# A retention-then-FFN kernel: one unit's transposes go from TensorE to the DMA queue, and loads, casts and a state sum change places

## The chip, the cores and the metric

The kernel runs on one core of a Trainium2 chip. The metric is the device time of one execution in microseconds. The kernel before was run three times: median 202.52 us, from 202.31 to 202.76. The profile shown comes from one further execution, which took 203.15 us; the span from its first to its last instruction is 201.4 us, so 1.75 us lie around the span.

A core has TensorE (matrix products, writes PSUM), VectorE (called DVE in the profile), ScalarE (ACT), GpSimd (POOL) and SyncE (SP, here used only to issue DMAs). POOL issues DMAs too: its queue is q0 in the profile, SP's is q1. The 16 DMA engines serve both. PSUM has 8 banks of 128 x 512 numbers in float32; the code writes each out by its number.

## The reference

A retention recurrence over 768 tokens, for 4 batches and 8 heads of size 64, and after it two matrix products with a PReLU between them, over all 4 x 768 = 3072 tokens:

```python
for t in range(S):
    state = gamma * state + einsum('bhd,bhe->bhde', k[:, :, t], v[:, :, t])
    y[:, :, t] = scale * einsum('bhd,bhde->bhe', q[:, :, t], state)
x = y.transpose(0, 2, 1, 3).reshape(3072, 512)
h = x @ w_in                                    # 512 x 2048
g = maximum(h, 0) + alpha * minimum(h, 0)
out = g @ w_out                                 # 2048 x 512
```

## The kernel before

**Units.** The recurrence is done in chunks. A unit is 256 tokens of one batch; there are 12, three to a batch, and two units make a block of 512 tokens for the FFN, so there are six blocks. A unit u goes through these steps, each a helper in the code:

- `load(u)` issues the DMAs of k, q and v on SP's queue into staging tiles `ks`, `qs`, `vs` (three buffers of each).
- `rescale(engine, u, t, h0, h1)` multiplies k (t=0) or q (t=1) of heads h0 to h1 by powers of the decay and writes `kdq` in float16. `cast_v` writes v in float16 as `vx`.
- `kdq` has tokens on the partitions; the scores need it turned. `turn_pe(u, hh, bank)` turns half of the heads with 8 TensorE transposes into a PSUM bank, and ACT copies the bank to `kq`. `turn_dma(u)` turns the whole `kdq` into `kq` with one transposing DMA on SP's queue. Units 0 to 3 use `turn_pe`, units 4 to 11 `turn_dma`.
- `score_mm(u, hh, banks)` makes the scores of half of the heads in two banks, `masks` (DVE) multiplies them by the causal mask into `m`, and thereby frees the banks.
- `sum_mm` makes the sums of k times v for each 128 tokens (tile `st`), `state_sum` (DVE, then POOL) adds one to the running state and applies the decay (tiles `ss`, `tf`), `state_copy` writes it in float16 as `tg` (ACT or POOL).
- `out_mm(u, banks)` makes the unit's output `y`: products of `tg` and `kq` (line 319) and of `m` and `vx` (line 339); `take_y` copies it to `xT`.

**FFN.** `ffn1(n, ...)` multiplies by w_in, turn after turn in the banks of its list, with ACT and DVE applying the PReLU (`hm`, then `gt`). For block 1 it is split: its first six turns need only unit 2 (the first 256 tokens), the later ones unit 3 too. Block 0 uses `ffn2`, which adds up w_out in four parts, one for each piece of w_out (`get_wo(0)` to `get_wo(3)`, cast on the way by DMAs that POOL issues). The later blocks use `ffn2_seven`, which makes the product from seven half-size ones (ox, oy, oz) and needs differences of w_out's quarters (`w_sums`, DVE) and of g's (`g_sums`, DVE).

**Order.** The schedule is manual: each engine runs its instructions in the order in which the code names them, and waits only for data or buffers. `ffn1` and `ffn2` are generators; `tick(gen, m)` issues the next m of their steps (matmuls, mostly), so the code weaves attention steps of the next units into the FFN. Dependencies beyond data are added by hand. `hold`, called by `load` for each whole DMA, makes the DMA wait for an instruction put on the list `held`. `behind` makes a POOL scaling wait for a named DVE instruction, the `gate`.

**Around the change** (lines 671 to 740, between the first FFN product of block 0 and the loop): POOL scales unit 2, then unit 2's scores, sums and masks are woven into `ffn2(0)`. Unit 3's load waits for the first mask of unit 2. The third piece of w_out is issued, and the load of unit 4 waits until it has landed. Unit 3 is scaled by DVE and POOL together, its v cast, and `turn_pe` for it stands inside the first half of `ffn1(1)`. The last w_out differences are the gate for the second scaling of unit 4; units 4 and 5 are then scaled and cast on POOL, and turned by DMA. In the loop, for u0 = 4, 6, ... the two units' sums and scores come first (lines 763 to 766), then the states and masks of u0 (767 to 772).

Of the kernel before, what the change touches and what calls it, by code (L numbers as in the profile page):

```python
# [21 lines left out]
def kernel(  # L22
# [106 lines left out]
    def load(u, parts="kqv"):  # L129
        b, c = divmod(u, UPB)  # L130
        t = staged.setdefault(u, {})
        for nm in parts:
            src = {"k": k, "q": q, "v": v}[nm[0]]
            if nm[0] not in t:
                t[nm[0]] = sbp.tile(
                    [128, H, 2 * D], FP, tag=f"{nm[0]}s", bufs=3, name=f"{nm[0]}s{u}"
                )
            h = slice(0, H) if len(nm) == 1 else slice(4 * int(nm[1]), 4 * int(nm[1]) + 4)
            if u >= SPLIT and nm != "q":
                for x in range(2):  # L140
                    for y in range(2):
                        at = U * c + 128 * x + 64 * y
                        nc.sync.dma_start(
                            out=t[nm][rows(x), :, D * y : D * y + D],
                            in_=src[b, :, at : at + 64, :].rearrange("h p d -> p h d"),
                        )
                continue
            hold(
                nc.sync.dma_start(  # L149
                    out=t[nm[0]][:, h, :],  # L150
                    in_=src[b, h, U * c : U * c + U, :].rearrange(
                        "h (p r) d -> p h (r d)", r=2
                    ),
                )
            )
# [10 lines left out]
    def rescale(eng, u, t, h0, h1):  # L166
        kdq = unit(u)[0]
        at = OQ if t else (O2 if u >= SPLIT else 0)
        return eng.tensor_tensor(  # L169
            out=kdq[:, t, :, h0:h1, :].rearrange("p r h d -> p h r d"),  # L170
            in0=staged[u]["kq"[t]][:, h0:h1, :].rearrange("p h (r d) -> p h r d", r=2),
            in1=tab[:, at + 2 * h0 : at + 2 * h1]
            .rearrange("p (h r) -> p h r", r=2)
            .unsqueeze(3)
            .to_broadcast([128, h1 - h0, 2, D]),
            op=MULT,
        )
# [115 lines left out]
    def masks(u, hh, parts=(0, 1)):  # L293
        for a in parts:
            m2 = sbp.tile([128, 512], F16, tag=f"m2{a}{hh}", bufs=2, name=f"m2{a}{hh}")
            if u >= SPLIT:
                i = nc.vector.tensor_tensor(
                    out=m2[:, 0:384], in0=live[u, hh][a][:, 0:384], in1=mj, op=MULT
                )
            else:  # L300
                i = nc.vector.tensor_tensor(  # L301
                    out=m2.rearrange("p (r a i) -> p r a i", r=2, a=2),
                    in0=live[u, hh][a].rearrange("p (r a i) -> p r a i", r=2, a=2),
                    in1=mask.unsqueeze(2).to_broadcast([128, 2, 2, 128]),
                    op=MULT,
                )
            live[u, hh][a] = m2
        return i
# [84 lines left out]
    def ffn1(n, banks, apart=0):  # L393


        gt = sbp.tile([128, NFT, TB], F16, tag="gt", bufs=2, name=f"gt{n}")
        gts[n] = gt
        turns = [(f, 2, ul, ul + 1) for ul in range(2) for f in range(0, apart, 2)]
        rest = range(apart, NFT)
        if apart == 0:  # L400
            rest = [f + x for f in range(HF) for x in (0, HF)]
        turns += [(f, 1, 0, 2) for f in rest]
        for i, (f0, nf, lo, hi) in enumerate(turns):
            hps = ps(banks[i % len(banks)], "hps").rearrange("p (f t) -> p f t", f=nf)
            for f in range(nf):
                for hp in range(4):
                    nc.tensor.matmul(  # L407
                        out=hps[:, f, :].rearrange("p (u t) -> p u t", t=U),
                        lhsT=w_in_all[:, hp, 128 * (f0 + f) : 128 * (f0 + f) + 128],
                        rhs=xT[n][:, lo:hi, hp, :],  # L410
                        start=(hp == 0),
                        stop=(hp == 3),
                    )
                    if f < nf - 1 or hp < 3:
                        yield
            hm = sbp.tile([128, TB], FP, tag="hm", bufs=3, name="hm")
            hm = hm.rearrange("p (f t) -> p f t", f=nf)
            nc.scalar.activation(out=hm, in_=hps, func=RELU, bias=0.0, scale=-1.0)  # L418
            for f in range(nf):
                nc.vector.scalar_tensor_tensor(  # L420
                    out=gt[:, f0 + f, U * lo : U * hi],
                    in0=hm[:, f, :],
                    scalar=oma_sb[:, f0 + f : f0 + f + 1],
                    in1=hps[:, f, :],
                    op0=MULT,
                    op1=ADD,
                )
            if n > 0 and f0 in ((HF + 3, NFT - 1) if apart == 0 else (NFT - 1,)):

                lo = 0 if apart or f0 < NFT - 1 else 4  # L430
                hi = HF if f0 == NFT - 1 else 4
                g_sums(n, 0, lo, hi)
                g_sums(n, 1, lo, hi)
            yield
# [146 lines left out]
    def get_wo(i):  # L581
        s = slice(4 * i, 4 * i + 4)
        return nc.gpsimd.dma_start(out=w_out_all[:, s, :], in_=wo[:, s, :])
# [88 lines left out]
    get_wo(1)  # L672
    rescale(G, 2, 1, 0, 4)
    rescale(G, 2, 0, 4, 8)
    rescale(G, 2, 1, 4, 8)
    cast_v(G, 2)
    out_mm(1, (4, 5), evict=False)
    take_y(1, (0,))
# [2 lines left out]


    gen = ffn2(0, (0, 1, 2, 3), parts=4)
    half = ffn1(1, (6, 7, 4, 5, 4, 6, 0, 1, 2, 3, 0, 4, 5, 6, 7, 1), apart=12)
    tick(gen, 5)
    turn_pe(2, 0, 5)
    tick(gen, 5)
    score_mm(2, 0, (6, 7))
    held.append(masks(2, 0, (0,)))
    load(3, ("k0", "q0", "k1", "q1", "v"))  # L690
    masks(2, 0, (1,))
    turn_pe(2, 1, 4)
    tick(gen, 6)
    score_mm(2, 1, (6, 7))
    sum_mm(2, (5, 4))
    state(2, 0, G, "ga")
    masks(2, 1)
    held.append(get_wo(2))
    load(4)
    load(5)  # L700
    rescale(V, 3, 0, 0, 4)
    rescale(G, 3, 1, 0, 4)
    get_wo(3)
    rescale(V, 3, 0, 4, 8)
    rescale(G, 3, 1, 4, 8)
    cast_v(G, 3)
    w_sums(0, 0, HF)
    tick(gen, 9)
    out_mm(2, (4, 5))
    tick(gen, 7)  # L710
    tick(half, 24)
    turn_pe(3, 0, 6)
    tick(half, 8)
    turn_pe(3, 1, 7)
    tick(half, 16)
    tick(gen, 9)
    score_mm(3, 0, (4, 5))
    masks(3, 0)
# [7 lines left out]
    for f in (0, 4):  # L726
        for i in range(1, 4):
            gate = w_sums(i, f, f + 4)
    behind(rescale(G, 4, 1, 0, 8), gate)
    rescale(G, 5, 0, 0, 8)  # L730
    rescale(G, 5, 1, 0, 8)
    cast_v(G, 4)
    cast_v(G, 5)
    tick(gen, 8)
    out_mm(3, (6, 7))
    tick(gen)
# [6 lines left out]
    for n in range(1, NBLK):  # L743
        more = n + 1 < NBLK
        u0 = 2 * (n + 1)
        if n > 1:
            gen = ffn1(n, (7, 2, 3, 1, 0, 6, 5, 4, 7, 1, 0, 4, 5, 6, 7, 1))
            if more:
                for u in (u0, u0 + 1):
                    i = rescale(G, u, 0, 0, 8)  # L750
                    if u == u0:
                        behind(i, gate)
                    rescale(G, u, 1, 0, 8)
                    turn_dma(u)
                    cast_v(G, u)
                    if u + 2 < NU:
                        load(u + 2)
                    tick(gen, 8)
            tick(gen)
        gen = ffn2_seven(n, 0, 1) if more else ffn2_seven(n, (0, 3), 1, 2)  # L760
        if more:
            tick(gen, 8)
            sum_mm(u0, (2, 3))
            sum_mm(u0 + 1, (2, 3), half=1)
            score_mm(u0, 0, (4, 5))
            score_mm(u0, 1, (6, 7))
            state(u0, 0, G)
            masks(u0, 0)
            s01 = state_sum(u0, 1, G)
            masks(u0, 1, (0,))  # L770
            s10 = state_sum(u0 + 1, 0, G)
            masks(u0, 1, (1,))
            tick(gen, 8)
            state_copy(s01, "aa")
            state_copy(s10)
            tick(gen, 17)
            if n == 1:
                load(7)
            state(u0 + 1, 1, G)
            g_sums(n, 2, 0, HF)  # L780
            tick(gen, 15)
            out_mm(u0, (4, 5))
            score_mm(u0 + 1, 0, (6, 7))
            score_mm(u0 + 1, 1, (2, 3))
            masks(u0 + 1, 0)
            masks(u0 + 1, 1)
            gate = g_sums(n, 3, 0, HF)
            tick(gen, 32)
            out_mm(u0 + 1, (4, 5))
        else:  # L790
            tick(gen, 33)
            g_sums(n, 2, 0, HF)
            g_sums(n, 3, 0, HF)
        tick(gen)
# [30 lines left out]
```

## Time and profile before

| | |
|---|---|
| median of three runs | 202.52 us |
| profiled execution | 203.15 us, of that span 201.4 us |
| TensorE busy (PE) | 193.2 us, 96% of the span |
| DVE busy | 155.3 us, 77% |
| ACT busy | 102.0 us, 51% |
| POOL busy | 85.1 us, 42% |
| granted TensorE clock | 1.000 |
| moved by DMA | 33.95 MB, 169 GB/s over the span |
| DMA transposes | 8, each 3.7 to 6.3 us from issue to landing |
| w_out's pieces | 4, each 6.1 to 10.3 us from issue to landing |

The profile gives busy time by engine, the chain of work that ended last (followed back from the last instruction, each piece with start and duration), waits (which engine was idle until which instruction or DMA was done), timelines of an engine, and DMA windows (packets and bytes by queue). Line numbers such as L199 are those of the kernel's code; a helper's line stands for all its uses, so the time and the tile's name tell which one is meant. `kq<-kdq` means an instruction that reads the tile `kdq` and writes `kq`. Idle time of an engine that isn't the bottleneck costs nothing by itself.

### The profile page before, as it was taken

The page shows a single profiled execution, that of the slowest core. Times are in us where ns is not written, and L with a number is a line of the kernel's source. Part 1 is how long each engine was busy: PE and PEld are TensorE (multiplying, and loading weights), DVE is VectorE, ACT ScalarE, POOL GpSimd, SP SyncE. Part 2 cuts the span into 40 slices and gives each one's busy share as a digit, 9 for nine tenths or more (in the row PEclk, how much of TensorE's full clock was granted, in tenths as well). Part 3 has the DMA queues.
Part 4 walks back from the last instruction along what each step waited for, and adds up shares of the span by engine and source line. Part 5 has one row for each costly group of instructions (what it writes and reads, how often), then busy time and mean ns, then how long its engine had stood idle before and what let it go on. Part 6 is the DMA issues. An engine that isn't in the chain of part 4 may idle for free.

```text
span 201.4 us, 5574 instructions
## 1 busy us (share of the span) xinstructions
PE 193.2 (96%) x2325; PEld 129.0 (64%) x2325; DVE 155.3 (77%) x251; ACT 102.0 (51%) x170; POOL 85.1 (42%) x99
## 2 busy tenths in 40 slices
PE   6896999999999999999999999999999999999993
PEld 2455644577467778744788644788544888544882
DVE  7695887657799999189997389994489984589851
ACT  2455776348276433477354377334476255466321
POOL 6189029282459463970076950176920250000000
PEclk9999999999999999999999999999999999999999
DMA  6999999499999997998976499992570011300014
GB/s 170 312 230 148 205 251 260 136 245 198 339 344 136 215 222 180 240 277 221 213 188 162 157 178 240 198 225 87 175 160 0 3 53 55 107 0 0 14 41 156
DMA packets 77561, 33.95 MB, mean 169 GB/s; under 512 B 43217, under 2 KB 77025, under 8 KB 77537
## 3 DMA queue, kind: packets, MB, share of 16 engines
q1 hardware_dynamic: 73136, 29.37, 56.8%
q0 software_dynamic: 4224, 4.19, 13.4%
q8 instruction: 18, 0.29, 0.6%
q10 hardware_dynamic: 176, 0.04, 0.1%
q14 instruction: 7, 0.05, 0.1%
HBM read 27.31 MB, written 6.29 MB: 167 GB/s over the span
## 4 chain that ended last, share of the span: by engine, by line
PE 86%; DMA 6%; DVE 2%; POOL 2%; SPq 1%; issue 1%; ACT 0%; POOLq 0%
PE hps L407 41%; PE ox L493 16%; PE oy L493 11%; PE ops L445 7%; DMA win<-in_moe_w_in_dram 4%; PE y L339 3%; DMA vs<-in_v_dram 3%; PE y L319 2%; PE sca L284 2%; SPq L149 1%; PE st L229 1%; PE trb L199 1%; PE oz L493 1%; DVE gs L391 1%; POOL tf L255 1%
## 5 line engine op out<-in xcount | busy, mean ns | idle before, releaser
L407 PE MATMUL hps<-xT,win 128*128 128x512 f16 (+1 forms) x448 | 84.7, 349 | 1.6 <-DMA win<-in_moe_w_in_dram 1.6
L420 DVE SCALAR_TENSOR_TENSOR gt<-hm,oma,hps 128x512 f16<-128x512 f32 (+1 forms) x112 | 71.1, 668 | 10.2 <-ACT hm L418 4.9
L418 ACT ACTIVATE hm<-hps 128x512 f32<-128x512 f32 x96 | 57.2, 597 | 32.2 <-PE hps L407 29.7
L407 PEld LDWEIGHTS <-win 128*128 128x128 f16 x448 | 43.5, 98 | 40.2 <-DMA win<-in_moe_w_in_dram 1.7
L493 PEld LDWEIGHTS <-gs 128*128 128x128 f16 x320 | 31.0, 98 | 3.8
L255 POOL TENSOR_TENSOR tf<-ss,tab 128x256 f32<-128x256 f32 x16 | 12.2, 764 | 36.2 <-DVE ss L254 35.3
L493 PEld LDWEIGHTS <-gt 128*128 128x128 f16 x240 | 22.8, 98 | 4.6
L509 ACT ACTIVATE cu<-ox 128x512 f32<-128x512 f32 (+1 forms) x18 | 9.5, 527 | 29.3 <-PE ox L493 29.2
L169 POOL TENSOR_TENSOR kdq<-ks,tab 128x1024 f16<-128x1024 f32 (+1 forms) x10 | 17.3, 1729 | 15.6 <-DMA ks<-in_k_dram 8.4
L514 DVE TENSOR_TENSOR os<-oy,cu 128x512 f32<-128x512 f32 x14 | 9.6, 689 | 17.2 <-PE oy L493 13.5
L169 POOL TENSOR_TENSOR kdq<-qs,tab 128x1024 f16<-128x1024 f32 (+1 forms) x13 | 21.3, 1641 | 2.8 <-issue 1.9
L270 POOL CAST tg<-tf 64x256 f16<-64x256 f32 x27 | 13.2, 491 | 19.6 <-DVE tf L251 18.3
L493 PE MATMUL ox<-wsum,gs 128*128 128x256 f16 x160 | 19.1, 273 | 0.0
L362 ACT ACTIVATE xT<-y 128x512 f16<-128x512 f32 x23 | 15.7, 743 | 6.0 <-PE y L339 5.8
L445 PE MATMUL ops<-wout,gt 128*128 128x512 f16 x64 | 15.3, 380 | 0.0
L185 POOL CAST vx<-vs 128x1024 f16<-128x1024 f32 (+1 forms) x13 | 12.5, 971 | 4.1 <-DMA vs<-in_v_dram 4.1
L391 DVE TENSOR_TENSOR gs<-gt 128x1024 f16<-128x1024 f16 (+1 forms) x14 | 13.1, 934 | 0.3
L268 ACT ACTIVATE tg<-tf 64x256 f16<-64x256 f32 x13 | 5.3, 414 | 14.0 <-POOL tf L255 9.0
L205 ACT ACTIVATE kq<-trb 128x1024 f16<-128x1024 f16 x8 | 8.2, 1024 | 7.1 <-PE trb L199 7.0
L301 DVE TENSOR_TENSOR m<-sca,mi 128x512 f16<-128x512 f32 x12 | 8.2, 687 | 3.4 <-PE scb L284 3.4
L493 PE MATMUL ox<-wout,gt 128*128 128x256 f16 x80 | 10.4, 274 | 0.0
L445 PEld LDWEIGHTS <-gt 128*128 128x128 f16 x64 | 5.8, 98 | 6.0
(55 smaller groups left out, 190.7 us busy)
## 6 DMA issues: line engine op xcount, KB each, us to landing
out_dram<-os SPq DMA_DIRECT2D x21, 256.0 KB, 3.0
qs<-in_q_dram SPq DMA_DIRECT2D x8, 512.0 KB, 5.7
ks<-in_k_dram SPq DMA_DIRECT2D x24, 128.0 KB, 3.5
vs<-in_v_dram SPq DMA_DIRECT2D x24, 128.0 KB, 4.8
ks<-in_k_dram SPq DMA_DIRECT2D x8, 256.0 KB, 4.8
qs<-in_q_dram SPq DMA_DIRECT2D x8, 256.0 KB, 5.1
win<-in_moe_w_in_dram POOLq DMA_DIRECT2D x4, 512.0 KB, 7.8
wout<-in_moe_w_out_dram POOLq DMA_DIRECT2D x4, 512.0 KB, 8.1
```

The lines of the kernel that those rows point to most:

```text
L169: return eng.tensor_tensor(out=kdq[:, t, :, h0:h1, :].rearrange("p r h d -> p h r d"), in0=staged[u]["kq"[t]][:, h0:h1, :].rearrange("p h ...
L185: eng.tensor_copy(out=o, in_=i)
L255: eng.tensor_tensor(out=t, in0=ss, in1=dec, op=MULT)
L270: nc.gpsimd.tensor_copy(out=o, in_=i)
L362: nc.scalar.activation(out=o, in_=i, func=COPY, bias=0.0, scale=1.0,)
L391: return nc.vector.tensor_tensor(out=o, in0=a, in1=b, op=op)
L407: nc.tensor.matmul(out=hps[:, f, :].rearrange("p (u t) -> p u t", t=U), lhsT=w_in_all[:, hp, 128 * (f0 + f) : 128 * (f0 + f) + 128], rhs=x ...
L418: nc.scalar.activation(out=hm, in_=hps, func=RELU, bias=0.0, scale=-1.0)
L420: nc.vector.scalar_tensor_tensor(out=gt[:, f0 + f, U * lo : U * hi], in0=hm[:, f, :], scalar=oma_sb[:, f0 + f : f0 + f + 1], in1=hps[:, f, :],
L445: nc.tensor.matmul(out=opss[tq], lhsT=gt[:, ft, 128 * tq : 128 * tq + 128], rhs=w_out_all[:, ft, :], start=(ft == 0), stop=(ft == NFT - 1),)
L493: nc.tensor.matmul(out=o[1][m], lhsT=lhs(f, m), rhs=rhs(f), start=(first and f == 0 and (m == 0 or o[0] is None)), stop=(f == HF - 1), ski ...
L514: nc.vector.tensor_tensor(out=so, in0=o[0], in1=t, op=ADD)
```

## The change

Four things are moved.

- Unit 3 is turned by one transposing DMA on SP's queue instead of sixteen TensorE transposes and two ACT copies. Its load is issued behind unit 2's last scaling instead of unit 2's first mask. On POOL, unit 3's two scalings, and the cast of its v, now come before the fourth piece of w_out. On SP, the transposing DMA stands between the load of unit 3 and those of units 4 and 5, which no longer wait for the third piece to land, only for their turn in the queue.
- The first half of block 1's `ffn1` is issued in one go, with 6 and 7 as the banks of its fifth and sixth turns, and the first w_out difference comes behind it on DVE.
- On POOL, the cast of unit 4 comes before the scaling that waits for the gate, and the cast of unit 5 between that unit's two scalings.
- In the loop, DVE masks the last part of u0's scores before it sums the first state of u0 + 1.

```diff
@@ -672,7 +672,8 @@
     get_wo(1)
     rescale(G, 2, 1, 0, 4)
     rescale(G, 2, 0, 4, 8)
-    rescale(G, 2, 1, 4, 8)
+    held.append(rescale(G, 2, 1, 4, 8))
+    load(3, ("k0", "q0", "k1", "q1", "v"))
     cast_v(G, 2)
     out_mm(1, (4, 5), evict=False)
     take_y(1, (0,))
@@ -681,38 +682,33 @@
     gen = ffn2(0, (0, 1, 2, 3), parts=4)
-    half = ffn1(1, (6, 7, 4, 5, 4, 6, 0, 1, 2, 3, 0, 4, 5, 6, 7, 1), apart=12)
+    half = ffn1(1, (6, 7, 4, 5, 6, 7, 0, 1, 2, 3, 0, 4, 5, 6, 7, 1), apart=12)
     tick(gen, 5)
     turn_pe(2, 0, 5)
     tick(gen, 5)
     score_mm(2, 0, (6, 7))
-    held.append(masks(2, 0, (0,)))
-    load(3, ("k0", "q0", "k1", "q1", "v"))
-    masks(2, 0, (1,))
+    masks(2, 0)
     turn_pe(2, 1, 4)
     tick(gen, 6)
     score_mm(2, 1, (6, 7))
     sum_mm(2, (5, 4))
     state(2, 0, G, "ga")
     masks(2, 1)
-    held.append(get_wo(2))
+    get_wo(2)
+    rescale(V, 3, 0, 0, 4)
+    rescale(G, 3, 1, 0, 4)
+    rescale(V, 3, 0, 4, 8)
+    rescale(G, 3, 1, 4, 8)
+    turn_dma(3)
     load(4)
     load(5)
-    rescale(V, 3, 0, 0, 4)
-    rescale(G, 3, 1, 0, 4)
+    cast_v(G, 3)
     get_wo(3)
-    rescale(V, 3, 0, 4, 8)
-    rescale(G, 3, 1, 4, 8)
-    cast_v(G, 3)
-    w_sums(0, 0, HF)
     tick(gen, 9)
     out_mm(2, (4, 5))
     tick(gen, 7)
-    tick(half, 24)
-    turn_pe(3, 0, 6)
-    tick(half, 8)
-    turn_pe(3, 1, 7)
-    tick(half, 16)
+    tick(half, 48)
+    w_sums(0, 0, HF)
     tick(gen, 9)
     score_mm(3, 0, (4, 5))
     masks(3, 0)
@@ -726,11 +722,11 @@
     for f in (0, 4):
         for i in range(1, 4):
             gate = w_sums(i, f, f + 4)
+    cast_v(G, 4)
     behind(rescale(G, 4, 1, 0, 8), gate)
     rescale(G, 5, 0, 0, 8)
+    cast_v(G, 5)
     rescale(G, 5, 1, 0, 8)
-    cast_v(G, 4)
-    cast_v(G, 5)
     tick(gen, 8)
     out_mm(3, (6, 7))
     tick(gen)
@@ -768,8 +764,8 @@
             masks(u0, 0)
             s01 = state_sum(u0, 1, G)
             masks(u0, 1, (0,))
+            masks(u0, 1, (1,))
             s10 = state_sum(u0 + 1, 0, G)
-            masks(u0, 1, (1,))
             tick(gen, 8)
             state_copy(s01, "aa")
             state_copy(s10)
```

## The prediction

> **What bounds the kernel now.** I read the page first, for the engine that sets the end, then the chain, for what runs on it around the change, then the rows of DVE, POOL, SP and the DMA queues that feed these places. The page's first part and two stretches of the chain:
>
> ```profile
> PE 193.2 (96%) x2325; PEld 129.0 (64%) x2325; DVE 155.3 (77%) x251; ACT 102.0 (51%) x170; POOL 85.1 (42%) x99
> ...
> 45.67 0.47 PE trb L199 x8
> ...
> 47.01 0.45 PE trb L199 x8
> ...
> 74.72 0.41 PE y L339 x15
> ```
>
> By the chain, TensorE works without a gap from 19.7 us to its last matmul at 198.3 but for one place: the rest of unit 4's `y` waits 0.43 us for a mask and starts at 74.72. So only two things are to be had: the 0.92 us of unit 3's sixteen transposes (0.47 + 0.45) and that 0.43 us. DVE's timeline shows where the mask comes from (start, duration, then in brackets idle time before):
>
> ```profile
> 72.74 0.68 DVE L301 TENSOR_TENSOR m<-sca,mi 128x512 f16<-128x512 f32 x1
> 73.65 0.42 DVE L254 TENSOR_TENSOR ss<-tf,st 128x256 f32<-128x256 f32 x1 [0.22 <-POOL tf L255]
> 73.98 0.68 DVE L301 TENSOR_TENSOR m<-scb,mi 128x512 f16<-128x512 f32 x1
> ```
>
> The last mask stands behind a state sum that waits for POOL. The queues, by the timelines of SP and POOL, the answer on kq and DMA windows (25 to 28 us, then 42 to 43.5):
>
> ```profile
> 36.69 0.37 SPq L149 DMA_DIRECT2D ks<-in_k_dram  x1
> ...
> 62.12 5.63 SPq L189 DMA_TRANSPOSE kq<-kdq  x2
> ...
> 40.06 0.81 POOL L583 DMA_DIRECT2D wout<-in_moe_w_out_dram  x1
> 40.89 1.06 POOL L169 TENSOR_TENSOR kdq<-qs,tab 128x512 f16<-128x512 f32 x1
> 41.88 0.81 POOL L583 DMA_DIRECT2D wout<-in_moe_w_out_dram  x1
> ...
> DMA to landing us min/median/max: 3.7/4.5/6.3
> ...
> q0 software_dynamic: 428, 0.43, 83.6%
> q1 hardware_dynamic: 430, 0.22, 35.5%
> ...
> q1 hardware_dynamic: 912, 0.46, 102.1%
> q0 software_dynamic: 15, 0.02, 8.0%
> ```
>
> The reader is to see that a DMA transpose lands 3.7 to 6.3 us after its issue, and that w_out's pieces (q0) and SP's transfers (q1) share evenly in one window and not at all in the other.
>
> **The change part by part.**
>
> *Transposes off TensorE.* 16 instructions, 0.47 + 0.45 = 0.92 us, all on the chain: -0.92. ACT loses two copies of 1.02 us; it was idle there, worth nothing. Everything TensorE needs after 47.5 is wanted 0.92 earlier.
>
> *load(3), held by unit 2's last scaling.* That scaling starts at 32.87 and lasts 1.04, so the five issues start at 33.95 instead of 36.69. SP has nothing else between 25.65 and 36.69. The DMA engines moved nothing from 36.0 to 37.5, so the loads fill a hole. Only w_out's second piece is in flight (issued 30.03, landed after 6.1, at 36.1); its user is the TensorE group at 38.37, 2.2 us later. Cost 0; bounds 0 to 0.5. The last q half landed at 38.20 + 5.2 = 43.4; 2.7 us sooner is 40.7.
>
> *POOL's order.* Third piece at 40.06 as before, scaling 40.89 to 41.95, second scaling to 43.0 (it took 1.92 before, beside the w_out difference that DVE ran at 43.30; that is moved away), cast 1.03 to 44.0, and only then the fourth piece, at 44.0 instead of 41.88. Its user is the 17th matmul of the last two parts: the eighth of the group at 51.78, 53.4, now 52.5. That allows 8.5 us; the four pieces took 6.1 to 10.3. I take 7 to 8: cost 0; bounds 0 and 10.3 - 8.5 = 1.8.
>
> *turn_dma(3) on SP.* It waits for the scalings, so issues at 43.0 and holds SP for 1.3 to 2.8 us. Behind it stand load(4), load(5) and block 0's four stores. load(4) comes at about 45.1 instead of 47.78, when the third piece had landed and let it go; that pays for the engines' time (66 to 68 us: 0.58 MB in 2 us, so 1.8 us for the 0.5 MB). Landing at 46.7 to 49.3; its user is score_mm(3,0), 51.15 - 0.92 = 50.2. Cost 0, cover 0.9 us at the longest row. The longest but one, 5.6, is the kernel's first transpose, whose engines moved 17 GB/s from 64 to 66 us; unit 3's will now be the first. Bounds 0 to 1.0 (rival 1). The third piece, alone on the engines from about 41.5, lands near 45, wanted at 48.3.
>
> *w_out's first difference behind the first half of ffn1(1).* 1.22 us of DVE. First-half evictions end near 49.85 (six groups of 0.87 from 44.6), the difference at 51.1; unit 3's first masks start 0.5 late and end at 52.4, while the scores that reuse their banks come at 53.61 - 0.92 = 52.7. Cost 0, cover 0.3. The bank list only frees 4 and 5 sooner: 0.
>
> *Casts sooner.* cast_v(5) ended at 67.79, just when sum_mm(5) wanted it; with TensorE 0.92 earlier it would have cost that much. It now ends near 64.5: 0. But cast_v(4) now lies beside w_out's later differences, 1.04 us of POOL. Such a difference takes 0.68 alone (58.77) and took 1.10 beside POOL's work (56.14), so DVE loses about 0.42, bounds 0 and 1.04; the forward end of unit 4's first scaling, 53.1 to 55.0, overlaps the first by another 0.1. DVE is busy without a gap from there to the masks, so they come about 0.4, not 0.92, sooner. turn_dma(4) follows the gate (60.05 - 0.4) and a 1.9 us scaling: issued 61.6, landed by 67.3 at the first's 5.6, and at 66.1 at the median; wanted at 67.4. Cost 0.
>
> Trainium skill, SBUF — State Buffer, "SBUF: two separate sides": a DVE operation with two SBUF inputs and a POOL operation that reads SBUF exclude each other for a whole instruction. The 1.10 row shows a loss of 0.42 of a possible 0.6, so neither full exclusion nor none. By the rule the cast would cost 1.04, the mask would be there at 74.25, and the sum below would be -0.45 instead of -1.05.
>
> *State sum behind the mask.* The masks follow each other at 0.6 us, so the last starts at 73.34, not 73.98, and ends at 74.03. The sum moves 0.4 later; it feeds unit 5, wanted at 79. With DVE 0.4 sooner, the mask is there at 73.6; TensorE wants it at 74.28 - 0.92 = 73.36. The wait is 0.43 before, 0.25 to 0.3 after: -0.15. In the two later blocks TensorE never waits there: 0.
>
> *Sum.* -0.92 - 0.15, call it -1.05; against this execution (203.15: span 201.4 and 1.75 around it) 202.1. The median of the runs is 0.63 lower: 202.52 - 1.05 = 201.5. The most to be had is -0.92 - 0.43 = -1.35, or 201.2.
>
> **The rivals.**
>
> *1. Unit 3's kq comes late.* 2,284 packets went in the 2 us after 66, all transpose and load pieces of 256 bytes, so one transpose is about 2,050. If it shares evenly with w_out's fourth piece as in the window at 25 us (428 packets in 3 us; a piece is 4,224 / 8 = 528, so 3.7 us), only 528 of its packets go in that time and the other 1,520 need 1.3 us. From its first packets (1.2 us after issue, 44.2), with the first transpose's 2 us pause, that is 51.2: TensorE waits 1.0. Sum -0.05, 202.5. For it: the even window and the pause. Against: the transpose starts 2 us before the fourth piece's first packets, and in the window at 42 us the queue that was there first ran on undisturbed. The Trainium skill, DMA: Bandwidth & Descriptors, "Queues, rings and completion order", has each DMA engine take turns between queues packet by packet, which is this rival; the first window agrees, the second doesn't.
>
> *2. The fourth w_out piece starves (the other side).* If q0 gets next to nothing while q1 is full, as at 42 to 43.5 us (15 packets against 912), the piece waits through unit 3's transpose and six loads of 0.5 MB, at 340 GB/s until about 57, and lands near 60: TensorE waits 7 us, 209. It makes the kernel slower from a landing after 53.6 on. For it: that window and the later issue. Against: the even window, and that the 42 us one may be no more than q0's start, 2 to 3 us after issue.
>
> *3. DVE gives the gain back.* With the cast excluding a difference in full (and the overlap of the scaling) DVE is 0.92 or more late and unit 4's mask stands still: ready at 74.03 to 74.2, wait 0.7 to 0.85: sum -0.5 to -0.65, 201.9. For it: DVE has no gap from 54 to 80 us. Against: 1.10 rather than 1.7 in the row.
>
> **How the numbers follow.** Forecast (201.2 to 201.7) 0.50; rival 1 with anything between 0.4 and 1.2 us of wait 0.19; rival 2 from just late to starved 0.15; rival 3 0.16. A measurement of this kernel tells about 0.2%, 0.4 us, from no change. Faster: 0.50 + most of rival 3 (0.11) + the short waits of rival 1 (0.04) = 0.65. Same: the rest of 3 (0.05) and most of 1 (0.11) = 0.16. Slower: rival 2 and the long waits of rival 1 (0.04) = 0.19. Range: from 201.0 (all of 1.35, and the runs' 0.2 of spread) to 203.2 (a wait of 1.7, near the fourth piece's longest row); beyond it stays most of rival 2.
>
> **What would show it.** Right: no transposes on TensorE for unit 3; TensorE without idle time between 45 and 55; kq lands before 50; the fourth piece before 52.4; a wait before unit 4's `y` of 0 to 0.4 us; everything after it some 1.05 us sooner. Wrong: TensorE waiting for kq at the scores near 50 (rival 1) or for wout at the ops near 52 (rival 2); the w_out differences stretched past 1.1 us beside the cast and the `y` wait at 0.6 or more (rival 3). The forecast falls if the pause of the first transpose is longer than 2 us with other transfers in flight.

## The result and the profile after

The changed kernel is slower: 1.0156 times the kernel before (95% interval 1.0129 to 1.0182), some 3.2 us, where 1.05 us less was forecast. Medians are 206.0 us over six runs and 202.4 us over six of the kernel before; the ratio leaves out three executions (two and one of them) in a second, slower state. The profiled execution took 208.7 us (span 207.0); its granted TensorE clock fell twice, once before 25 us and once after the wait shown below. The first fall, behind a wait of 2.8 us for w_in (1.6 before), belongs to this execution: TensorE's first `ops` group begins 2.62 us later (35.49 instead of 32.87), ahead of all that the change touches but the load. So times of TensorE in the two profiles are compared with 2.6 us taken off, and the account goes from that group on. The last run below has a second profile of the changed kernel without that first fall.

By the chains, from the first `ops` group to the end of the last one it was 32.87 to 58.34 = 25.5 us before and 35.49 to 64.32 = 28.8 us after: 3.4 us more. From there to the last matmul it was 139.9 us and is now 139.5: 0.4 us less. All that is lost is lost in the first stretch. The page and the chain of the changed kernel (start, duration, what):

```profile
PE 194.8 (94%) x2309; PEld 129.2 (62%) x2309; DVE 158.7 (77%) x251; ACT 100.3 (48%) x168; POOL 84.5 (41%) x99
...
PE 82%; DMA 10%; DVE 4%; SPq 1%; POOL 0%; issue 0%; ACT 0%; POOLq 0%; DVEq 0%
...
42.72 4.99 DVE kdq L169 x2
...
47.85 7.61 DMA kq<-kdq
...
56.20 3.16 PE ops L445 x8
```

TensorE has 16 instructions fewer, and the chain now leaves it: two DVE scalings, then the transposing DMA, then eight matmuls that take 3.16 us where the same eight took 1.83. The timelines of DVE, POOL and SP around it, and the wait:

```profile
42.64 5.06 DVE L169 TENSOR_TENSOR kdq<-ks,tab 128x512 f16<-128x512 f32 x2
...
43.51 2.05 POOL L169 TENSOR_TENSOR kdq<-qs,tab 128x512 f16<-128x512 f32 x2
45.50 1.03 POOL L185 CAST vx<-vs 128x1024 f16<-128x1024 f32 x1
46.48 0.80 POOL L583 DMA_DIRECT2D wout<-in_moe_w_out_dram  x1
...
47.85 4.89 SPq L189 DMA_TRANSPOSE kq<-kdq  x1
...
PE sca L284 <- DMA kq<-kdq: 2.6, 1, 2.6
```

The first of the two DVE scalings takes 4.45 us instead of 0.68; it ends at 47.09, 0.55 us after the end of POOL's cast. Only then does the second run, in 0.68, and behind it the transpose is issued, at 47.85; it lands 7.6 us later, at 55.46, with TensorE idle since 52.86. While it was pending, the third piece of w_out was in flight until 49.2 us and the fourth until 52.9. The DMA windows of 48 to 51 and of 52.5 to 54 us show the queues one after the other, POOL's q0 first (packets, MB, share):

```profile
q0 software_dynamic: 359, 0.37, 100.4%
...
q1 hardware_dynamic: 1541, 0.39, 120.6%
```

And the windows of the stretch (us; busy time of PE, PEld, DVE, ACT, POOL; granted clock; DMA) show what follows the wait:

```profile
52.90:55.50 2.60, 0.00 (x0) 0.00 (x0) 1.05 (x1) 0.00 (x0) 0.00 (x0) 1.00 0.96 224
55.50:57.50 2.00, 2.00 (x53) 1.14 (x54) 1.53 (x3) 0.00 (x0) 0.00 (x0) 0.76 1.15 342
57.50:59.40 1.90, 1.90 (x9) 0.50 (x11) 0.09 (x1) 0.41 (x1) 1.74 (x2) 0.50 1.15 347
```

The clock is granted in full while TensorE idles here, and halves after work is back: a mean of 0.76 over 2 us, between 1.00 and 0.50, puts the fall some 1 us behind the end of the wait. So the 3.4 us are: -0.92 for the transposes, +2.64 wait, +1.33 for eight matmuls at half clock, and 0.3 in the small instructions next to them.

Three theories came out of this. A: DVE is shut out by POOL as long as POOL's instructions follow each other without a gap. B: the transposing DMA is late because of POOL's w_out pieces on the same DMA engines, whenever it is issued. C: the slow matmuls come from the idle time.

### The profile page after: what moved, and what is told of

The parts are those of the page before. It is cut to its first block, busy times and chain, and to the rows that moved or that the text cites. A ratio compares the mean times of both kernels' runs of the same rounds, so it can differ in the third digit from the quotient of the medians.

```text
span 207.0 us, 5537 instructions
## 1 busy us (share of the span) xinstructions
PE 194.8 (94%) x2309; PEld 129.2 (62%) x2309; DVE 158.7 (77%) x251; ACT 100.3 (48%) x168; POOL 84.5 (41%) x99
## 4 chain that ended last, share of the span: by engine, by line
PE 82%; DMA 10%; DVE 4%; SPq 1%; POOL 0%; issue 0%; ACT 0%; POOLq 0%; DVEq 0%
PE hps L407 38%; PE ox L493 17%; PE oy L493 12%; PE ops L445 5%; DMA win<-in_moe_w_in_dram 4%; DMA kq<-kdq 4%; DMA vs<-in_v_dram 3%; DVE kdq L169 2%; PE y L339 2%; PE y L319 2%; PE sca L284 2%; PE st L229 1%; SPq L149 1%; PE oz L493 1%; DVE m L301 1%; PE trb L199 0%
## 5 line engine op out<-in xcount | busy, mean ns | idle before, releaser
L255 POOL TENSOR_TENSOR tf<-ss,tab 128x256 f32<-128x256 f32 x16 | 11.3, 709 | 40.0 <-DVE ss L254 38.6
L493 PEld LDWEIGHTS <-gt 128*128 128x128 f16 x240 | 22.8, 98 | 4.6
L270 POOL CAST tg<-tf 64x256 f16<-64x256 f32 x27 | 14.1, 521 | 23.0 <-DVE tf L251 21.7
L169 POOL TENSOR_TENSOR kdq<-qs,tab 128x1024 f16<-128x1024 f32 (+1 forms) x13 | 20.4, 1574 | 1.3 <-DVE wsum L378 1.2
L445 PE MATMUL ops<-wout,gt 128*128 128x512 f16 x64 | 16.7, 405 | 0.0
L284 PE MATMUL sca<-kq 64*64 64x128 f16 (+1 forms) x192 | 8.0, 216 | 3.9 <-DMA kq<-kdq 2.6
L284 PEld LDWEIGHTS <-kq 64*64 64x64 f16 x384 | 6.0, 109 | 7.3 <-ACT kq L205 3.4
```

The source lines that it names most:

```text
L169: return eng.tensor_tensor(out=kdq[:, t, :, h0:h1, :].rearrange("p r h d -> p h r d"), in0=staged[u]["kq"[t]][:, h0:h1, :].rearrange("p h ...
L255: eng.tensor_tensor(out=t, in0=ss, in1=dec, op=MULT)
L270: nc.gpsimd.tensor_copy(out=o, in_=i)
L284: nc.tensor.matmul(out=scs[a][rows(c), at : at + n], lhsT=kv[rows(a), 0, r, p, rows(c)], rhs=q, start=True, stop=True,)
L445: nc.tensor.matmul(out=opss[tq], lhsT=gt[:, ft, 128 * tq : 128 * tq + 128], rhs=w_out_all[:, ft, :], start=(ft == 0), stop=(ft == NFT - 1),)
L493: nc.tensor.matmul(out=o[1][m], lhsT=lhs(f, m), rhs=rhs(f), start=(first and f == 0 and (m == 0 or o[0] is None)), stop=(f == HF - 1), ski ...
```

## The experiments

Each was timed beside the kernel before on the same chip; ratios are to that.

**All four scalings of unit 3 on DVE.**

```diff
-    rescale(G, 3, 1, 0, 4)
+    rescale(V, 3, 1, 0, 4)
     rescale(V, 3, 0, 4, 8)
-    rescale(G, 3, 1, 4, 8)
+    rescale(V, 3, 1, 4, 8)
```

> Unit 3's four scalings all on DVE (the q halves taken off POOL), the rest as in the changed kernel. Theory A (DVE's scaling, which took 4.45 us instead of 0.68, was shut out by POOL's unbroken row of scaling, scaling, cast): the scalings take 0.68 each except at most one that meets POOL's cast, the transposing DMA is issued some 4 us sooner, unit 3's kq lands before the scores want it, TensorE has no wait of 2.6 us there: 201.1 to 201.7 us, about 4 us under the changed kernel. Theory B (the transposing DMA is late because of what else is on the DMA engines, whenever it is issued): it lands 7 us or more after issue, TensorE still waits 0.5 to 2 us: 202 to 204 us.

Measured: 1.0009 (0.9955 to 1.0062). DVE's timeline, the wait, and the DMA windows 41.6 to 43.9, 45.5 to 46.9 and 47.1 to 48.9 us:

```profile
38.91 0.68 DVE L169 TENSOR_TENSOR kdq<-ks,tab 128x512 f16<-128x512 f32 x1
39.51 0.68 DVE L169 TENSOR_TENSOR kdq<-qs,tab 128x512 f16<-128x512 f32 x1
...
PE sca L284 <- DMA kq<-kdq: 1.4, 1, 1.4
...
q0 software_dynamic: 406, 0.42, 113.0%
...
q1 hardware_dynamic: 1393, 0.36, 113.5%
...
q0 software_dynamic: 347, 0.36, 121.8%
```

The shut-out is gone: four scalings of 0.68, and the transpose is issued at 41.54. But it waits for the third piece, moves its data, and is reported landed only at 50.4, 8.9 us after issue, when the fourth piece is nearly through as well (it landed at 50.7), though no packet of q1 went from 47.1 to 48.9. A and B are both at work; 1.4 us of wait are left with DVE out of the picture.

**The turn back on TensorE**, and the load of unit 4 held by the third piece again; the rest as changed.

```diff
-    get_wo(2)
+    held.append(get_wo(2))
...
-    turn_dma(3)
...
-    tick(half, 48)
+    tick(half, 24)
+    turn_pe(3, 0, 6)
+    tick(half, 8)
+    turn_pe(3, 1, 7)
+    tick(half, 16)
```

(and the bank list of before).

> The changed kernel with unit 3 turned on TensorE again (sixteen transposes, old bank list), and the load of unit 4 held by the third piece of w_out again; early load of unit 3, POOL's order, casts and state sum stay changed. Theory A and B alike: no wait for kq; the 0.43 us wait before unit 4's y is gone; the long DVE scaling is still there (A: about 4 us) and costs TensorE at most 0.3 us through late evictions or transposes: 202.0 to 202.3 us. If the wait for kq was not the loss, it stays near 205.6.

Measured: 1.0007 (0.9966 to 1.0048). The loss goes with the DMA turn. What was expected of the rest, a gain of 0.1 to 0.4 us, isn't seen: TensorE waits elsewhere, for evictions that come behind w_out's differences. In that profile these take 5.77 us from the first to the next eviction, instead of 4.44:

```profile
PE hps L407 <- DVE gt L420: 0.4, 1, 0.4
```

**Idle matmuls in the wait.**

```diff
     tick(gen, 9)
+    keep(12, 4)
     score_mm(3, 0, (4, 5))
```

> The changed kernel with twelve idle matmuls of 512 columns (2.6 us at full clock) put before unit 3's first scores, where TensorE waits for kq. If TensorE's slow eight matmuls after the wait (3.16 us instead of 1.83) come from having been idle, they run in 1.8 us and the kernel gains 1.2 to 1.6 us: 204.0 to 204.5. If they come from something else (late w_out, the DMA), nothing changes: 205.4 to 206, or up to 0.5 more where the matmuls outlast the wait.

The twelve added matmuls have a result that nobody uses. Measured: 1.008 (1.004 to 1.0121), about half of the changed kernel's loss, and kq landed later still, 8.6 us after issue, so that TensorE idled 0.9 us behind the idle matmuls. By the chain the eight matmuls behind the wait:

```profile
53.91 1.83 PE ops L445 x8
```

They run at full speed, which is theory C. Waits of 1.4 us (all scalings on DVE) and 2.1 us (the run with the queues in turn, below) left the clock at 1.00 too. One of 2.1 us in the next run, those of 2.6 in both profiles of the changed kernel, and the later ones of 3.6 and 3.9 did not. When it falls varies: by the windows' means 0.3 us after work is back in the next run, 1.6 us after it behind the wait of 3.6, and 2.5 us into the wait of 3.9, with TensorE still idle.

**The early load alone, in the kernel before.**

```diff
-    rescale(G, 2, 1, 4, 8)
+    held.append(rescale(G, 2, 1, 4, 8))
+    load(3, ("k0", "q0", "k1", "q1", "v"))
...
-    held.append(masks(2, 0, (0,)))
-    load(3, ("k0", "q0", "k1", "q1", "v"))
-    masks(2, 0, (1,))
+    masks(2, 0)
```

> The kernel before with one part of the change alone: unit 3's load issued behind unit 2's last scaling. Theory A: with all of its data there early, POOL's row (scaling, scaling, cast) is unbroken and DVE's first scaling is shut out until it ends, 4 us or more instead of 0.68; the w_out difference and the evictions behind it come 2 us late, TensorE waits 0.5 to 2 us for banks or for unit 3's kdq: 202.9 to 204.5. Theory B: the scalings take 0.7 us each, time unchanged within 0.3 us of 202.4.

Measured: 1.0033 (0.9981 to 1.0085), by itself no verdict. Its profile shows the mechanism (DVE, POOL, the wait):

```profile
39.82 5.75 DVE L169 TENSOR_TENSOR kdq<-ks,tab 128x512 f16<-128x512 f32 x2
...
42.51 1.06 POOL L169 TENSOR_TENSOR kdq<-qs,tab 128x512 f16<-128x512 f32 x1
43.50 1.51 POOL L185 CAST vx<-vs 128x1024 f16<-128x1024 f32 x1
...
PE trb L199 <- DVE gt L420: 2.1, 1, 2.1
```

The first scaling takes 4.30 us and ends 0.55 us after POOL's second scaling; the evictions behind it on DVE come late and TensorE waits 2.1 us. So the early load can bring the shut-out by itself. This execution took 206.9 us, the others between 202.3 and 207.2, so the wait of 2.1 us isn't in all of them.

In the kernel before, POOL's scalings were waiting for their data when DVE's were ready: q's halves landed at 40.3 and 43.4, DVE's scalings began at 40.02 and 42.69. The end of the long scaling lies 0.55 to 0.56 us after the end of a POOL instruction in all six profiles that have one (changed kernel twice, 47.09 and 46.54 in the first; this run; the turn on TensorE; idle matmuls; the run with POOL's scalings and the late piece). How long it lasts goes with how far POOL's row was ready. In the turn on TensorE it took 2.49 us, as q's second half landed only at 40.8, when POOL's first scaling ended; with the idle matmuls 3.48, as v landed at 42.5, when POOL's second scaling ended. In the kernel before DVE used the 0.8 us in which POOL only issues a DMA; with POOL's next instruction ready it did not. One row doesn't fit theory A: in this run POOL's cast had its v from 41.8 on, and DVE still got in before it.

The Trainium skill, SBUF — State Buffer, "SBUF: two separate sides", has a DVE operation with two SBUF inputs and a POOL operation that reads SBUF exclude each other for a whole instruction, with the one that starts first going ahead. The traces agree that they exclude each other, but not on who goes ahead: in the changed kernel DVE's scaling began at 42.64 and POOL's first at 43.51, and DVE's waited, through three POOL instructions.

**The fourth piece issued later**, behind the evictions of the third turn; all scalings on DVE.

```diff
     cast_v(G, 3)
-    get_wo(3)
...
     tick(half, 48)
+    behind(get_wo(3), marks[1, 2])
```

> As the run with all four scalings on DVE, but the fourth piece of w_out is issued only when DVE has written the evictions of the third turn of the first half (some 4 us later). Theory B, sharpened by the runs so far (SP's transfers and POOL's pieces don't interleave: whichever came later waits until the other's whole piece is through, and a transpose's last small packets, which report it done, queue again): with nothing of POOL's queue behind the transpose, kq lands 6 to 6.5 us after issue instead of 8.9, TensorE's wait of 1.4 us is gone, and the fourth piece still lands in time: 201.0 to 201.6, 0.8 to 1.3 us under the kernel before. Rival (the transpose is slow by itself, being the first, with its pause): it lands 8 us or more after issue again and the wait stays 1 us or more: 202.2 to 203.

Measured: 1.0111 (1.0075 to 1.0146). The transpose does what was expected, the piece doesn't (landing of kq; the wait; window 46.5 to 51 us, where q0 has no packet):

```profile
DMA to landing us min/median/max: 5.1/5.1/5.1
...
PE ops L446 <- DMA wout<-in_moe_w_out_dram: 3.6, 1, 3.6
...
q1 hardware_dynamic: 3227, 1.24, 108.4%
```

The first half of theory B holds: with no piece behind it the transpose lands 5.1 us after issue and nobody waits. But now the piece, issued at 47.24, comes after the load of unit 4 (46.17) and has no packet for 3.8 us: the prediction's rival 2. Some 1.5 us of that are a piece's ordinary start: the third piece of the changed kernel, issued at 42.69 onto idle engines, had its first packets at 44.

**The same with POOL's scalings as in the change.** The edit is the one above, on the changed kernel.

> The changed kernel with the fourth piece of w_out issued as late as in the run before, but POOL's two scalings left where the change has them. DVE's first scaling is shut out for 2.5 to 4.5 us as before, so the transpose is issued 2 to 4 us later than with all scalings on DVE; kq then lands 5 to 7 us after issue, TensorE waits 0 to 1.5 us: 201.5 to 203.3. It says what the shut-out alone costs, without the queue. If both causes are needed for the loss, no wait at all and 201.0 to 201.6.

Measured: 1.0229 (1.0193 to 1.0265). DVE's first scaling takes 4.46 us, the transpose is issued at 44.76, lands after 4.8 us, and no wait for kq is left; TensorE waits 3.9 us for wout instead:

```profile
PE ops L446 <- DMA wout<-in_moe_w_out_dram: 3.9, 1, 3.9
```

The wait for kq can now be read off four cases: 2.6 us with the shut-out and the piece (the changed kernel), 1.4 with the piece alone (all scalings on DVE), none with the shut-out alone (this run), none with neither (the run before). The piece has to be there for a wait, and the shut-out's 3.8 us make it longer; only with both did the clock fall behind it. The times of this run and the one before can't show this, since the late piece makes a wait of its own.

**The queues in turn**: all scalings on DVE, the fourth piece behind the second turn's evictions, the load of unit 4 behind the fourth turn's, the cast of unit 5 after its scalings.

```diff
     tick(half, 48)
+    piece = get_wo(3)
+    behind(piece, marks[1, 1])
+    held.append(marks[1, 3])
+    load(4)
+    load(5)
```

> All of the change's aims with the causes found taken away: unit 3's four scalings on DVE, and the two queues in turn: the fourth piece of w_out issued behind the evictions of the second turn (after the transpose has been handed over), the load of unit 4 behind those of the fourth turn; the cast of unit 5 after its scalings, so that unit 5's transpose isn't delayed. If first come, first served between the queues and the shut-out of DVE explain the loss, kq lands 5 to 6 us after issue, the piece lands before its part begins, TensorE waits less than 0.3 us in all: 201.0 to 201.6, 0.8 to 1.4 us under the kernel before. If a wait of 0.5 to 1.5 us stays (for wout or for unit 4's scaled k), the time is 201.6 to 203.

Measured: 1.0058 (1.0022 to 1.0095), above what was expected. Landing, the waits:

```profile
DMA to landing us min/median/max: 10.2/10.2/10.2
...
PE sca L285 <- DMA kq<-kdq: 2.1, 1, 2.1
...
PE ops L446 <- DMA wout<-in_moe_w_out_dram: 0.4, 1, 0.4
```

The third piece dragged on to 47.5 us. The transpose, begun before that was done, moved next to nothing from 45 to 47, where both queues together had 125 packets, and it was reported landed at 51.7, near the end of the fourth piece; from 49 to 50.5 q1 had no packet.

**The load of unit 4 behind the piece's landing**: the same with `held.append(piece)`.

> The same, but the load of unit 4 waits until the fourth piece has landed. The piece has the DMA engines to itself: no wait for wout for certain; the loads of units 4 and 5 end 1 to 3 us later than in the kernel before, so POOL's scalings of units 4 and 5 and their transposes may come late: 201.0 to 201.6 if they have slack, 202 to 203 if unit 4's kq or unit 5's v is then late.

Measured: 1.016 (1.0099 to 1.022), above what was expected as well. kq landed after 4.9 us; the piece was still 1.0 us late for TensorE, and the loads came so late (55.3 us) that TensorE later waited for unit 5's v:

```profile
PE st L230 <- POOL vx L186: 2.6, 1, 2.6
```

**The state sum alone, and with the casts, in the kernel before.**

```diff
             masks(u0, 1, (0,))
+            masks(u0, 1, (1,))
             s10 = state_sum(u0 + 1, 0, G)
-            masks(u0, 1, (1,))
```

> The kernel before with one part alone: the last mask before the sum of the next unit's first state. If the 0.43 us before unit 4's y is only the order of two DVE instructions, the wait goes and 0.4 us with it: 0.3 to 0.5 us under the kernel before. If something else is late next (the state sum, wanted by the scores that reuse its bank), less than 0.2.

Measured: 0.9983 (0.9966 to 1.0000), 0.34 us less; its profile has no wait before unit 4's `y`. It comes out furthest ahead of all versions, and its interval ends at no difference.

> The kernel before with the state sum behind the mask and the casts of units 4 and 5 sooner, nothing else. If casts beside w_out's differences stretch these (one took 1.5 us instead of 0.68 in the changed kernel) and TensorE then waits 0.3 to 0.4 us for a bank, as in the run with the turn on TensorE, the gain of the state sum is lost: within 0.15 us of the kernel before. If the stretch is hidden: 0.3 to 0.5 us under it.

Measured: 0.9998 (0.997 to 1.0026), which can't tell 0.3 us from nothing. In its profile the difference beside unit 4's cast takes 1.52 us instead of 0.68, but TensorE waits neither for a bank nor before unit 4's `y`; what the casts cost stays open, below the noise.

**The changed kernel again.**

> The changed kernel once more, on the chip of these runs: the first profile of it had the lower granted clock from its wait of 2.6 us on. Expected: the wait for kq of 2 to 3.5 us again, DVE's first scaling of unit 3 at 2.5 to 4.5 us, 1.3 to 1.8% over the kernel before. If the clock falls again only behind a wait of over 2 us, the fall is the wait's.

Measured: 1.0193 (1.0118 to 1.0269). The first scaling takes 4.45 us, kq lands 7.6 us after issue, TensorE waits 2.6 us, and the clock falls to 0.51 behind it, all as in the first profile. Here the first `ops` group begins at 33.00, 0.13 us from the kernel before, and from it to the end of the last one are 28.9 us, again 3.4 more than before. The fall isn't in every execution: of the first six, the mean granted clock was 0.982 to 0.991 in five and 1.000 in the fastest, of 204.7 us. In this profile TensorE waited for unit 7's kq too, 2.9 us at 107.8: that transpose took 7.2 us to land with no w_out piece in flight, so such a piece isn't the only thing that can make one late. In the first profile it landed after 5.6 us; the reason stays open.

## Why the prediction was wrong

*Transposes off TensorE, -0.92.* Right: sixteen instructions fewer, and the two groups are gone.

*load(3), cost 0, bounds 0 to 0.5.* Right on the DMA side: the loads did fill the hole, and the last q half landed at 39.7 in the second profile, even before the 40.7 of the prediction. But here the prediction failed first. The early data made POOL's row ready at the same time as DVE's scalings; the lateness of the load had kept the two engines apart. The prediction asked who waits for the loads sooner, and not which two engines would then run side by side. It had the rule of the exclusion at hand and applied it to the casts only, where it cost nothing in the end.

*turn_dma(3), issued at 43.0, landing 46.7 to 49.3, cost 0.* Wrong in both halves, and the step that decides. The 43.0 is the end of POOL's second scaling, and that came out: 45.56 - 2.6 = 42.9. DVE's two scalings, for which the transpose waits as well, had no term; they ended at 47.70 instead of some 43.9 (two of 0.68 from 42.64 on), so the issue came at 47.85 - 2.6 = 45.2, 2.2 us late. The landing took 7.6 us, outside 3.7 to 6.3, and up to 10.2 in other runs: the rows for it came from transposes that had no w_out piece beside them. The cover was said to be 0.9 us and the worst case 1.0; the wait was 2.64. The earlier load(4), which was to pay for the engines' time, didn't come: it was put at 45.1 and came at 50.2 on the same clock, since the transpose held SP for 4.89 us instead of 1.3 to 2.8. And in the kernel before the 16 engines were already busy almost without a gap from 37.5 to 61 us (share 1.06); each other order tried made something else late, wout, unit 5's v or kq.

*Rival 1* had the place (kq late at the first scores) and the reason (the w_out piece on the same engines), but not the form. Its reason against, that the transpose starts 2 us before the piece's first packets, fell with the shut-out: the piece was issued at 46.48 and the transpose at 47.85. In the windows shown the queues don't share evenly: the one that is there first goes through, as in the prediction's second window. That the report of the transpose's end then queues once more is what two runs suggest (all scalings on DVE, and the queues in turn), where it landed 2.8 us and more after the last of its some 2,050 small packets. Nor did the prediction price what a long wait does to the clock, 1.3 us and more. The Trainium skill, TensorE: Matmul & The Clock Gate, "HAM oscillation — how this bites in real kernels", has the clock drop behind idle gaps of over about 3.4 us; here 2.6 was enough in both profiles of the changed kernel and 2.1 in the early load alone, while 2.1 with the queues in turn was not.

*The last sign of being wrong*, a pause of the transpose of over 2 us with other transfers in flight, was about reached in one run only, from 45 to 47 us with the queues in turn; with the late piece and all scalings on DVE it was some 1 us.

*Rival 2*, the starving piece, didn't occur in the changed kernel, where the piece is issued before the transpose, but in the two runs that issue it later, with waits of 3.6 and 3.9 us; some 3 us of these are the later issue itself (47.24 against 43.98 in the second profile).

*POOL's order, w_out's first difference.* Cost 0 as said in that nothing waited for the fourth piece or for the masks. But the new order also made POOL's row one without a gap, though the early load alone shows that the shut-out doesn't need it. *Casts.* A difference beside the cast took 1.52, not 1.10: 0.84 more instead of 0.42, which is the exclusion nearly in full. TensorE saw nothing of it in the changed kernel, since DVE caught up over the following evictions; rival 3 didn't happen there, a wait of 0.4 did in the run with the turn on TensorE.

*State sum, -0.15.* Right in kind and better in size: the wait of 0.43 is gone altogether, and the run with that part alone gained 0.34 us, within its interval.

## What to carry to other kernels

Before a load or a result is made to come sooner, ask which engines its lateness kept apart: work that ran one after the other may now meet on a port, and one engine may stand still through several instructions of the other. A transposing DMA may be priced from rows of the same kernel only where the same traffic lies beside it; where the DMA engines are already busy without a gap, expect a new transfer to make another one late, as every order tried here did. And a wait of 2 to 3 us on TensorE can cost more than itself.

## What the runs showed of the hardware that was not expected

- DVE's scaling of 128x512 in float32 with two SBUF operands: 0.68 us alone, 1.52 to 4.46 beside POOL instructions that read SBUF, ending 0.55 us after the end of one of them.
- A transposing DMA on SP's queue beside w_out pieces from POOL's: 7.6, 7.6, 8.6, 8.9 and 10.2 us to landing, and 4.06 to 5.88 us of SP to issue; the same one with no piece behind it 4.8, 4.9 and 5.1, and 2.65 to 2.9 to issue. Of the later ones, with no piece in flight, one took 7.2.
- The granted clock fell to 0.5 some 1 us and 0.5 us after TensorE had resumed from waits of 2.6 us (the two profiles of the changed kernel), and stayed there for some 3 us.
